# Batch 0 of a fused attention and MLP kernel reworked: head sets and token halves, one PSUM tile placed by hand, W_in products by chunks, a new step order

## Chip, core and metric

The kernel runs on one core of a Trainium2 chip. The metric is the device time of one execution in microseconds (us); less is better. The kernel before took 251.21 us (median of three runs, 250.34 to 251.27).

## What is computed

Eight batches, eight heads, 576 tokens, head width 64, 32 packed rows per head. Inputs are float32, the output is a float32 array of 4608 x 512.

```
def sm_attn(qq, kk, vv):
    s = scale * np.matmul(qq, kk.transpose(0, 1, 3, 2))
    a = np.exp(s - max)
    a = a / (np.sum(a, axis=-1, keepdims=True) + 1e-09)
    return np.matmul(a, vv)
p_packed = sm_attn(p, k, v)              # 32 rows per head
out = sm_attn(q, p_packed, p_packed)     # 576 rows per head
x = out.transpose(0, 2, 1, 3).reshape(4608, 512)
g = s * np.maximum(x @ w_in, 0) ** 2 + b     # w_in 512 x 2048
return g @ w_out                             # w_out 2048 x 512
```

## The kernel before, in words

Everything is computed in bf16 with float32 sums in PSUM. x is never formed: per batch the packed rows (ppd) are multiplied by W_in (tile pw, made by `packed_w`), and the normalised second attention weights (aT) are multiplied by pw, which gives the hidden layer at once.

Per batch the steps are, by the words of the step string: L* loads; T or D transposes (T on TensorE, D by DMA); V reorders V; F the first scores and their exponentials; P the packed rows; X their transposition; S the second scores and exponentials; A the sums, logarithm, inverse and product that give aT; W the product ppd by W_in (16 small matmuls for two chunks of 512 columns, in tiles of 64 x 32 of the array); M (16 per batch, four matmuls of 288 columns each) the hidden layer, relu on ScalarE (ACT) and square on VectorE (DVE); O the output products, 16 matmuls of 512 columns for each 128 tokens, then one DVE instruction and the stores. Batch 0 uses half steps (h, G, E) for its first M. Z and Y are matmuls on zeros that compute nothing (56 in all). BT and BC make the bias row from the column sums of W_out.

The order of every engine is written out by hand: each instruction is pinned to program order, so the step string (lines 660 to 689) and the prologue (633 to 658) fix the order on TensorE (PE), DVE, ACT, GpSimd (POOL) and SyncE (SP). POOL issues the casting loads, SP the stores and the DMA transposes. `mm` is line 62, `tr` line 65, and all of DVE, ACT, POOL and SP go through line 73, so the profile's lines name helpers and tiles tell more.

PSUM before: two pools, `psh` (tag h, two buffers of two banks, `big()`) and `psy` (tag y, four buffers of one bank). A buffer is taken in rotation when the tile is made. Loads of batch 0 (`load`, lines 115 to 122) are cut by heads 0 to 3 and 4 to 7. `first_scores` works on the head sets a = 0 (even heads) and a = 1 (odd heads), so its first half needs both cuts of K. `bias_sums` leaves its four partial rows in biasrep, and `bias_rows` adds them with a float32 matmul.

```
mm(where[a, x][NP * g:NP * g + NP], ppd[b % 2][D * a:D * a + D, a, g, :],
   w_in_sb[D * a:D * a + D, g, ch * NB:(ch + 1) * NB], ..., tile_position=(D * a, NP * g))
```

Of the kernel before, what the change touches and what calls it, by code (L numbers as in the profile page):

```python
# [7 lines left out]
F32 = mybir.dt.float32  # L8
# [6 lines left out]
def kernel(  # L15
# [32 lines left out]
    JJ = NP // 16  # L48

    constp = ctx.enter_context(tc.tile_pool(name="constp", bufs=1))  # L50
    rawp = ctx.enter_context(tc.tile_pool(name="rawp", bufs=1))
    attp = ctx.enter_context(tc.tile_pool(name="attp", bufs=1))
# [5 lines left out]
    psh = ctx.enter_context(tc.tile_pool(name="psh", bufs=2, space=bass.MemoryType.PSUM))  # L58
    psy = ctx.enter_context(tc.tile_pool(name="psy", bufs=4, space=bass.MemoryType.PSUM))
# [17 lines left out]
    early = []  # L77

    def big(dt=F32):
        if early:  # L80
            return early.pop()
        return psh.tile([P, 2, NB if dt == F32 else 2 * NB], dt, tag="h", name="hps")
# [12 lines left out]
    pn = [constp.tile([P, 2, 2, D], BF16, name=f"pn{i}") for i in range(2)]  # L95
    pall = constp.tile([16 * (B - 2), 16, 2, D], BF16, name="pall")
# [10 lines left out]
    rowsf = constp.tile([P, P], F32, name="rowsf")  # L107
# [7 lines left out]
    def load(what, b, h0=0, h1=H):  # L115
        src = {"k": k, "q": q, "v": v}[what]
        if h0 == 0:
            raw[what, b] = rawp.tile([R, H, NC * D], BF16, tag=what + "n", name=what + "n")
        pool.dma_start(
            out=raw[what, b][:, h0:h1, :],  # L120
            in_=src[b, h0:h1].rearrange("h (r c) d -> r h (c d)", c=NC),
        )

# [20 lines left out]

    def load_sb():
        sp.dma_start(out=svec[:], in_=moe_s[0:1].unsqueeze(0).to_broadcast([P, 1]))
        sp.dma_start(out=bvec[:], in_=moe_b[0:1].unsqueeze(0).to_broadcast([P, 1]))
# [6 lines left out]

    def prep_p(b):
        pt = big(BF16)
        for x in range(2):
            tr(
                pt[:, 0, x * P:(x + 1) * P],
                pn[b][:, x, :, :],  # L160
                identb[:],
            )
        for c2 in range(2):
            act.copy(
                out=pbd[D * c2:D * c2 + D, :, b, :, c2, :],
                in_=pt[D * c2:D * c2 + D, 0, 0:2 * P].rearrange("p (g a j) -> p a g j", g=4, a=2),
            )

    def prep_pall():
        n = 16 * (B - 2)  # L170
        pts = [psy.tile([P, 8 * P], BF16, tag="y", name="pps") for _ in range(2)]
# [6 lines left out]
        for x in range(2):  # L178
            src = pts[x][:].rearrange("p (t n) -> p t n", n=P)[:, :, 0:n].rearrange(
                "p t (x a i) -> p a x i t", a=2, i=JJ  # L180
            )
            for c2 in range(2):
                for a in range(2):
                    out = pbd[D * c2:D * c2 + D, a, 2:B, :, c2, :].rearrange(
                        "p b g (i t) -> p (b g) i t", i=JJ
                    )[:, :, :, 8 * x:8 * x + 8]
                    (act.copy if x else vec.tensor_copy)(out=out, in_=src[D * c2:D * c2 + D, a])

    def on_pe(b, what, half):
# [3 lines left out]
        tpw = big(BF16)  # L193
        tp = [tpw[:, 0], tpw[:, 1]]
        split = b == 0 and what == "q"
        if split:
            tp[1] = psy.tile([P, 2 * NB], BF16, tag="y", name="tps")
        for h4 in range(4):
            for cp in range(CP):
                o = (h4 % 2) * HS + cp * R  # L200
                tr(
                    tp[h4 // 2][:, o:o + R],
                    raw[what, b][:, 4 * half + h4, cp * P:(cp + 1) * P],
                    identb[0:R, 0:R],
                )
        d = dst[:, half * 4 * HS:(half + 1) * 4 * HS].rearrange("p (a s) -> p a s", a=2)
        if split:
            act.copy(out=d[:, 0], in_=tp[0][:, 0:2 * HS])
            vec.tensor_copy(out=d[:, 1], in_=tp[1][:, 0:2 * HS])
        else:  # L210
            vec.tensor_copy(out=d, in_=tpw[:, :, 0:2 * HS])
# [8 lines left out]
    def order_v(b, h0=0, h1=H):  # L220
        vec.tensor_copy(
            out=vr[:, :, h0:h1, 0:D].rearrange("r c h d -> r h c d"),
            in_=raw["v", b][:, h0:h1, :].rearrange("r h (c d) -> r h c d", c=NC),
        )

    def first_scores(b, a):
        if a == 0:
            e1[b] = attp.tile([R, 2, NC, 4, NP], BF16, tag="e1", name="e1")
        s1 = big()
        for g in range(4):  # L230
            for cp in range(CP):
# [8 lines left out]
                )  # L240
        act.activation(
# [8 lines left out]
    def packed(b, half=None):  # L250

        if not half:
            pps[b] = psy.tile([P, NB], F32, tag="y", name="pps")
        pp = pps[b][:, 0:2 * DV].rearrange("p (a x) -> p a x", a=2)
        for a in range(2):
            for c in range(NC):
                for g in range(4) if half is None else (2 * half, 2 * half + 1):
# [8 lines left out]
        if half == 0:  # L266
            return
        rd = smp.tile([P, 2], F32, tag="rd", name="rd")
        vec.reciprocal(out=rd[:], in_=pp[:, :, D])
        pk[b] = smp.tile([P, 2, 2, D], BF16, tag="pk", name="pk")  # L270
        for a in range(2):
# [6 lines left out]
    def turned(b):  # L278

        pt = pps[b][:, NB // 2:].bitcast(BF16)  # L280
        for a in range(2):
            tr(pt[:, a * P:(a + 1) * P], pk[b][:, a].rearrange("p c d -> p (c d)"), identb[:])
        vec.tensor_copy(
            out=ppd[b % 2][:].rearrange("p a g j -> p (a g j)"),
            in_=pt[:, 0:2 * P],
        )

    def second_scores(b, by_half=False, with_w=False):
        e2[b] = attp.tile([P, 2, S], BF16, tag="e2", name="e2")
        tiles = [big() for _ in range(2)]  # L290
        for a in range(2):
            for g in range(4):
                for c2 in range(2):
                    t, i = (c2, a) if by_half else (a, c2)
                    mm(
                        tiles[t][NP * g:NP * g + NP, i, 0:HS],
# [6 lines left out]
        if by_half:  # L303
            exp_half(b, tiles, 0, 0)
            exp_half(b, tiles, 1, 0)
            s2[b] = tiles
            return
        if with_w:
            packed_w(b, [0])
        for a in range(2):  # L310
            act.activation(
# [6 lines left out]
    def exp_half(b, tiles, a, hf):  # L318
        act.activation(
            out=e2[b][:, a, hf * HS:(hf + 1) * HS],  # L320
            in_=tiles[hf][:, a, 0:HS],
# [4 lines left out]
    def weights_half(b, hf):  # L326
        if hf == 0:
            aT[b] = atp.tile([P, 2, S], BF16, tag="aT", name="aT")
        dps = big()
        for a in range(2):  # L330
            mm(dps[:, a, 0:HS], onesbd[:], e2[b][:, a, hf * HS:(hf + 1) * HS], start=True, stop=True)
        if hf == 0:
            exp_half(b, s2[b], 0, 1)
            exp_half(b, s2[b], 1, 1)
        ld = smp.tile([P, 2, HS], F32, tag="ld", name="ld")
        act.activation(out=ld[:], in_=dps[:, :, 0:HS], func=AF.Ln)
        rcd[hf] = smp.tile([P, 2, HS], F32, tag="rcd", name="rcd")
        act.activation(out=rcd[hf][:], in_=ld[:], func=AF.Exp, scale=-1.0)

    def weigh_half(b, hf):  # L340
        cols = slice(hf * HS, (hf + 1) * HS)
        vec.tensor_tensor(out=aT[b][:, :, cols], in0=e2[b][:, :, cols], in1=rcd[hf][:], op=ALU.mult)

    def weights(b, a):
        if a == 0:
            aT[b] = atp.tile([P, 2, S], BF16, tag="aT", name="aT")
        dps = big()
        for hf in range(2):
            mm(dps[:, hf, 0:HS], onesbd[:], e2[b][:, a, hf * HS:(hf + 1) * HS], start=True, stop=True)
        ld = smp.tile([P, 2, HS], F32, tag="ld", name="ld")  # L350
        act.activation(out=ld[:], in_=dps[:, :, 0:HS], func=AF.Ln)
        rc = smp.tile([P, S], F32, tag="rcd", name="rcd")
        act.activation(out=rc[:], in_=ld[:].rearrange("p a s -> p (a s)"), func=AF.Exp, scale=-1.0)
        vec.tensor_tensor(out=aT[b][:, a, :], in0=e2[b][:, a, :], in1=rc[:], op=ALU.mult)

    def packed_w(b, chs):
        if b not in pw:
            pw[b] = atp.tile([P, 2, DFF], BF16, tag="pw", name="pw")
        where = {}
        if len(chs) > 1:  # L360
            pair = [big() for _ in range(2)]
            where = {(a, x): pair[a][:, x, :] for a in range(2) for x in range(2)}
        if len(chs) != 2:
            single = [psy.tile([P, NB], F32, tag="y", name="wps") for _ in range(2)]
            where.update({(a, len(chs) - 1): single[a][:] for a in range(2)})
        for x, ch in enumerate(chs):
            for g in range(4):
                for a in range(2):
                    mm(
                        where[a, x][NP * g:NP * g + NP],  # L370
                        ppd[b % 2][D * a:D * a + D, a, g, :],
                        w_in_sb[D * a:D * a + D, g, ch * NB:(ch + 1) * NB],
                        start=True,
                        stop=True,
                        tile_position=(D * a, NP * g),
                    )
        if len(chs) > 1:
            for a in range(2):
                dst = pw[b][:, a, chs[0] * NB:(chs[0] + 2) * NB].rearrange("p (i f) -> p i f", f=NB)
                evict(dst, pair[a][:], a == 0)  # L380
        if len(chs) != 2:
            ch = chs[-1]
            if b == 0 and ch == 0:
                s2["w"] = single
# [336 lines left out]
```

The softmax here doesn't subtract the row's maximum and nothing guards it: scores larger than these inputs give would overflow.

## Time and profile before

| what | value |
| --- | --- |
| time, median of three runs | 251.21 us |
| span of the profiled execution, first to last instruction | 248.04 us (no other time is recorded for that execution; its distance to the median is 3.17 us) |
| busy: PE, DVE, ACT, POOL | 241.6, 144.4, 140.6, 29.1 us |
| granted TensorE clock, mean | 1.000 |
| DMA: bytes, software queue, hardware queue | 35.50 MB, 18.61 MB, 16.49 MB |
| matmuls on zeros | 56 of 2302 |

How to read it: PE is the matmul row and PEld the weight load that overlaps it. A matmul's listed duration (for instance 380 ns for 128x512) includes its way through the array; consecutive ones start closer together, so costs on PE are read from the distance of starts in the timeline. The chain of waits follows the last instruction back to what released each step. A DMA's landing is its issue time on POOL or SP plus the time to landing in the view of DMA issues.

### The profile page before, as it was taken

To read this page: it belongs to the slowest core of one execution; us is meant where nothing else is said; L and a number is where in the kernel's file an instruction comes from. 1 tells how busy PE (TensorE), PEld (TensorE's weight loads), DVE (VectorE), ACT (ScalarE), POOL (GpSimd) and SP (SyncE) were. 2 spreads that over 40 slices of the span, in tenths; PEclk is the share of its full clock that TensorE was granted. 3 is DMA by queue.
4 is the path that set the end of the run, shared out by engine and by line. 5 is a ranking of instruction groups with operands and counts; after the bars stand their busy time and mean duration, and the time that the engine had idled before them with its cause. 6 is when DMAs were issued, how large, how long until landed. Compare 5 with 4: busy or idle time off the path is not lost.

```text
span 248.0 us, 5518 instructions
## 1 busy us (share of the span) xinstructions
PE 241.6 (97%) x2302; PEld 134.2 (54%) x2302; DVE 144.4 (58%) x278; ACT 140.6 (57%) x218; POOL 29.1 (12%) x43
## 2 busy tenths in 40 slices
PE   8999899999999999999999999999999999999994
PEld 2655565356644665456544654466545654366453
DVE  4438875599564864386538753586348742767221
ACT  2266742558837772758555953888266844578000
POOL 8733212000300012000300030000200000000000
PEclk9999999999999999999999999999999999999999
DMA  6999999999696589939798999337998811121133
GB/s 74 174 206 208 201 203 204 197 204 162 136 213 140 140 138 144 225 89 193 115 209 169 160 147 226 85 80 156 146 230 133 185 37 50 42 46 42 42 87 86
DMA packets 59450, 35.50 MB, mean 143 GB/s; under 512 B 32160, under 2 KB 54944, under 8 KB 59424
## 3 DMA queue, kind: packets, MB, share of 16 engines
q0 software_dynamic: 25184, 18.61, 50.8%
q1 hardware_dynamic: 34192, 16.49, 30.2%
q8 instruction: 18, 0.29, 0.5%
q14 instruction: 8, 0.07, 0.1%
q10 hardware_dynamic: 48, 0.03, 0.0%
HBM read 37.23 MB, written 9.44 MB: 188 GB/s over the span
## 4 chain that ended last, share of the span: by engine, by line
PE 82%; DMA 16%; issue 1%; POOL 0%; DVE 0%; POOLq 0%
PE yps L62 49%; PE hps L62 31%; DMA w_out_sb<-in_moe_w_out_dram 14%; DMA kn<-in_k_dram 2%; PE pps L62 1%; PE pps L65 1%; POOL kn L73 0%; DVE ysb L73 0%; POOL identb L73 0%; POOLq L73 0%; POOLq L705 0%
## 5 line engine op out<-in xcount | busy, mean ns | idle before, releaser
L62 PE MATMUL yps<-w_out_sb,gT 128*128 128x512 bf16 (+1 forms) x592 | 147.8, 374 | 0.6 <-DMA w_out_sb<-in_moe_w_out_dram 0.6
L73 ACT ACTIVATE rlu<-hps 128x576 bf16<-128x576 f32 x124 | 77.0, 649 | 23.1 <-PE hps L62 19.9
L62 PEld LDWEIGHTS <-gT 128*128 128x128 bf16 x592 | 54.8, 98 | 50.9 <-issue 8.8
L62 PE MATMUL hps<-aT,pw 128*128 128x288 bf16 x512 | 78.3, 285 | 0.2 <-ACT rlu L73 0.2
L73 DVE TENSOR_TENSOR gT<-rlu 128x576 bf16<-128x576 bf16 x128 | 57.8, 457 | 26.1 <-ACT rlu L73 23.3
L62 PEld LDWEIGHTS <-pw 128*128 128x128 bf16 x512 | 49.7, 97 | 26.3 <-issue 1.2
L73 DVE SCALAR_TENSOR_TENSOR ysb<-yps,svec,biasrep 128x512 f32<-128x512 f32 (+1 forms) x37 | 27.0, 733 | 21.7 <-PE yps L62 21.5
L73 ACT ACTIVATE e<-hps 96x768 bf16<-96x768 f32 (+2 forms) x34 | 21.8, 693 | 30.8 <-PE hps L62 30.6
L73 ACT CAST pw<-hps 128x1024 bf16<-128x1024 f32 x14 | 14.2, 1012 | 21.6 <-PE hps L62 21.0
L73 DVE TENSOR_TENSOR aT<-e,rcd 128x576 bf16<-128x576 bf16 x16 | 12.1, 757 | 23.4 <-ACT rcd L73 23.2
L73 POOL DMA_DIRECT2D kn<-in_k_dram x9 | 6.9, 767 | 130.1 <-DMA kT<-kn 97.8
L73 DVE CAST pw<-hps 128x1024 bf16<-128x1024 f32 x14 | 17.1, 1220 | 4.7 <-PE hps L62 4.6
L62 PE MATMUL zps<-zb 128*128 128x512 bf16 x42 | 13.6, 452 | 1.2 <-DVE zb L73 1.2
L73 ACT ACTIVATE rcd<-ld 128x576 f32<-128x576 f32 x16 | 10.9, 683 | 0.5
L73 ACT ACTIVATE ld<-hps 128x576 f32<-128x576 f32 x16 | 10.3, 643 | 1.2 <-PE hps L62 0.4
L62 PEld LDWEIGHTS <-ppd 64*32 64x32 bf16 x384 | 3.8, 88 | 11.0 <-issue 8.1
L62 PEld LDWEIGHTS <-zb 128*128 128x128 bf16 x56 | 5.6, 108 | 7.2 <-issue 3.2
L73 DVE RECIPROCAL rd<-pps 128x2 f32<-128x2 f32 x8 | 1.4, 171 | 13.3 <-PE pps L62 13.3
L62 PE MATMUL hps<-w_in_sb,ppd 64*32 64x512 bf16 x224 | 8.9, 381 | 0.0
L62 PEld LDWEIGHTS <-kT 128*128 128x128 bf16 x192 | 6.9, 98 | 2.5 <-issue 0.5
L73 DVE COPY vr<-vn 96x3072 bf16<-96x3072 bf16 (+1 forms) x9 | 8.0, 893 | 0.1
L73 POOL DMA_DIRECT2D vn<-in_v_dram x9 | 6.7, 751 | 5.5 <-DVE vr L73 2.9
(58 smaller groups left out, 104.0 us busy)
## 6 DMA issues: line engine op xcount, KB each, us to landing
out_dram<-ysb SPq DMA_DIRECT2D x23, 192.0 KB, 2.6
kn<-in_k_dram POOLq DMA_DIRECT2D x7, 576.0 KB, 7.1
vn<-in_v_dram POOLq DMA_DIRECT2D x7, 576.0 KB, 10.7
qn<-in_q_dram POOLq DMA_DIRECT2D x7, 576.0 KB, 13.3
out_dram<-ysb SPq DMA_DIRECT2D x24, 128.0 KB, 2.4
w_in_sb<-in_moe_w_in_dram POOLq DMA_DIRECT2D x4, 512.0 KB, 14.3
w_out_sb<-in_moe_w_out_dram POOLq DMA_DIRECT2D x4, 512.0 KB, 18.7
out_dram<-ysb SPq DMA_DIRECT2D x23, 64.0 KB, 2.1
```

Source lines behind the costliest of these rows:

```text
L62: return tc.keep_in_program_order(nc.tensor.matmul(*a, **kw))
L65: return tc.keep_in_program_order(nc.tensor.transpose(*a, **kw))
L73: return lambda *a, **kw: tc.keep_in_program_order(f(*a, **kw))
```

## The change

Six parts, made together:

1. **PSUM**: the two pools give way to one tile of eight banks, `banks`, and each step names the bank that it takes behind an @ in the step string. Dependencies are still kept by bank.
2. **Batch 0**: K and V are loaded by head sets (even heads, then odd ones) and Q by token halves (two tiles of 48 partitions); K's transposes, V's reordering, P and X go by sets; Q's transposes, S, the sums, logarithms and products by token half and set. The eight pieces of W_in's product of batch 0 have 256 columns each.
3. **W_in**: its first 256 columns come as float32 on ACT's hardware queue into a buffer of pw and are cast in two parts (C0, C1); P of batch 0 comes as float32 on SP's queue. The other columns come as 512, 256, 512 and 512.
4. **W by chunks**: the product of batches 1 to 7 takes one chunk of 512 columns at a time (8 matmuls, two banks, an eviction of 512 columns on either engine).
5. **Bias**: four partial rows are added by DVE on 32 partitions and scaled into biasrep; the float32 matmul is gone. s and b are loaded by POOL, late.
6. **Order**: a new step string of some 1125 words. Every step with a matmul is begun by one word and carried on by repeated words (a on ACT, v on DVE), so evictions stand apart from the matmuls in it; O has up to four output tiles open at once, and Q is its eviction. 44 matmuls on zeros remain.

```
+    banks = psp.tile([P, 8, NB], F32, name="banks")
+    spots = []
+    def take(n, dt=F32):
+        x = spots.pop(0)
+        t = banks[:, x:x + n, :]
+        return t if dt == F32 else t.bitcast(dt)
...
+    def load_part(what, part):
+        if what == "q":
+            raw["q", 0, part] = rawq.tile([R0, H, NC * D], BF16, tag="qn", name="qn")
...
+            in_={"k": k, "v": v}[what][0].rearrange("(g a) (r c) d -> a r g (c d)", a=2, c=NC)[part],
...
+    def load_w0():
+        wf = atp.tile([P, 2, DFF], BF16, tag="pw", name="pw")
...
+        act.dma_start(out=raw["w"], in_=moe_w_in[:, 0:256].rearrange("(k p) f -> p k f", p=P))
+    def cast_w0(x):
+        to((yield), w_in_sb[:, 2 * x:2 * x + 2, 0:256], raw["w"][:, 2 * x:2 * x + 2])
...
+    def packed_w0(c0, c1):
+        t = take(2)
+        n = c1 - c0
+        for g in range(4):
+            for a in range(2):
+                mm(
+                    t[NP * g:NP * g + NP, a, 0:n],
...
+        for a in range(2):
+            to((yield), pw[0][:, a, c0:c1], t[:, a, 0:n])
...
     def prep_pall():
-        pts = [psy.tile([P, 8 * P], BF16, tag="y", name="pps") for _ in range(2)]
+        pts = [take(1, BF16)[:, 0] for _ in range(2)]
...
-                    (act.copy if x else vec.tensor_copy)(out=out, in_=src[D * c2:D * c2 + D, a])
+                    to((yield), out, src[D * c2:D * c2 + D, a])
...
     def bias_sums():
+        yield
+        vec.tensor_copy(out=bias4[:], in_=ps[0:NP, 0, :])
+        for g in range(1, 4):
+            vec.tensor_tensor(out=bias4[:], in0=bias4[:], in1=ps[NP * g:NP * g + NP, 0, :], op=ALU.add)
+        for g in range(4):
+            vec.tensor_scalar_mul(out=biasrep[NP * g:NP * g + NP], in0=bias4[:], scalar1=bvec[0:NP])
...
-        Lwi0 Lwi1 Lwo0 Lwi2 Lwi3 Lwo1 Lp1 Tk0.0 Z10 PD Tk0.1 Lk1 PP0 Z3 F0.0 V0.0 F0.1 Z5 P0.0 V0.1 Lv1
-        P0.1 Z1 Tq0.0 Z1 X0 Z1 Tq0.1 Lq1 Lwo2 Lwo3 Lpall Z3 S0 Z3 A0.0 Z1 W0.0 A0.1 G0.0 E Y8 h0.0.0
...
+        PD0 C0 Z3@6 PP0@1 PP0a Z7@0 Tk0.0@2 Tk0.0a C0v Lq0.1 Tk0.0a PP0v Z6@0 Tk0.1@4 Tk0.1v Tk0.1a V0.0
+        F0.0@6 F0.1@0 F0.0 F0.1 Lp1 Z2@5 P0.0@2 P0.0 Z3@6 X0.0 X0.0a V0.1 Z1@0 P0.1 P0.1 Z1@0 Tq0.0@3,4
+        Tq0.0v Tq0.0v X0.1 Z2@0 Tq0.1@3,5 Tq0.1a C1 C1v S0.0.0@6 X0.1v S0.0.1 e0.0 PD1 e0.1 PP1@4 W0.0@0
+        Tq0.1v S0.1.0@2 S0.1.1 PP1v PP1v e1.1 Z2@5 d1.1@4 W0.0v e1.0 d0.1@6 l1.1 i1.1 d0.0 Lwi2.4 d1.0
+        l1.0 i1.0 Lwi1.2 W0.0v W0.3@0 W0.3v l0.0 Z4@2 W0.1@2 W0.3v W0.2@4 G1.1 l0.1 i0.0 G1.0 Z1@0
+        h0.6.1@0 W0.1a W0.2a W0.1v h0.2.1@6 W0.2v h0.6.1v i0.1 h0.0.1@2 h0.2.1a Lwi4.6 G0.0 G0.1 h0.0.1a
+        Lwi6.8 W0.5@4 W0.5v W0.5a Lk1 Lv1 h0.6.1 h0.2.1 h0.0.1 W0.4@0 W0.4v h0.2.0@6 h0.2.0a h0.10.1@2
...
+        Tq1.1a Tq1.1v W1.0@2 S1@6,4 W1.0a W1.0v Lsb S1 W1.1@0 W1.1v W1.1v W1.3@2 h0.4.0 PA O0.0x1@6
+        h0.8.1 S1 O0.1x1@7 O0.0x3 A1.1@4 W1.3v W1.3a O0.2x1@0 A1.1 O0.2x1 O0.3x2@1 A1.1 Lk2 O0.3x1
+        O0.2x1 A1.1 PPA0@4,5 O0.1x1 Lwo8.12 A1.0@2 PPA0v O0.1x1 PPA0a O0.0x3 PPA0v O0.2x1 O0.3x1 PPA0v
+        O0.3x1 A1.0 W1.2@2 O0.2x1 PPA0v A1.0 h0.12.1 Dk2 PPA0a PPA0v PPA0a W1.2a O0.3x2 A1.0 M1.3@4
+        M1.3a W1.2v O0.1x1 O0.2x1 M1.11@2 M1.9@4 M1.11a M1.9v O0.2x1 Lwo12.16 M1.9 Lv2 O0.1x3 M1.3
+        M1.0@2 M1.0a M1.10@4 M1.10a M1.11 O0.0x1 Lq2 O0.2x1 BT@2 M1.2@4 M1.2a O0.2x4 M1.0 O0.2x2 M1.14@4
+        O0.2x1 M1.14a BT Dq2 O0.1x3 F2.0@2 F2.0 O0.3x1 F2.1@4 F2.1 V2 O0.3x2 M1.2 Lq3 O0.2x1 Q0.2 M1.6@2
...
```

## Prediction

> **What bounds the kernel now.** I read the page first: busy shares, slices, clock and chain.
>
> ```profile
> span 248.0 us, 5518 instructions
> ...
> PE 241.6 (97%) x2302; PEld 134.2 (54%) x2302; DVE 144.4 (58%) x278; ACT 140.6 (57%) x218; POOL 29.1 (12%) x43
> ...
> PE   8999899999999999999999999999999999999994
> ...
> PEclk9999999999999999999999999999999999999999
> ...
> PE yps L62 49%; PE hps L62 31%; DMA w_out_sb<-in_moe_w_out_dram 14%; DMA kn<-in_k_dram 2%; PE pps L62 1%; PE pps L65 1%; POOL kn L73 0%; DVE ysb L73 0%; POOL identb L73 0%; POOLq L73 0%; POOLq L705 0%
> ```
>
> PE is the bound, full in every slice, at full clock. But 14% of the chain is the load of W_out: PE's early work ends up waiting for DMA. So what counts is when useful work starts, what PE issues, and when W_out is there. Next the timeline of PE up to 50 us.
>
> ```profile
> 1.19 5.30 PE L62 MATMUL zps<-zb 128*128 128x512 bf16 x12 [1.19 <-DVE zb L73]
> ...
> 20.37 0.65 PE L62 MATMUL hps<-aT,pw 128*128 128x288 bf16 x4
> ...
> 27.85 0.41 PE L62 MATMUL wps<-w_in_sb,ppd 64*32 64x512 bf16 x8 [0.57 <-DMA w_in_sb<-in_moe_w_in_dram]
> ...
> 42.35 0.59 PE L62 MATMUL yps<-w_out_sb,gT 128*128 128x512 bf16 x2 [0.57 <-DMA w_out_sb<-in_moe_w_out_dram]
> ...
> 44.89 1.05 PE L62 MATMUL hps<-w_out_sb,onesb 128*32 128x512 bf16 x16
> 45.87 0.42 PE L62 MATMUL hps<-e,onesbd 128*128 128x288 bf16 x2
> ...
> 47.47 1.10 PE L62 MATMUL hps<-biasrep,rowsf 128*128 128x512 f32 x2
> 48.40 1.03 PE L62 MATMUL yps<-w_out_sb,gT 128*128 128x512 bf16 x4
> ```
>
> The first M stands at 20.37; two waits for loads follow; BT, which needs all of W_out, ends at 45.87 (the start of the next matmul). From there PE never rests. Last, the end, in the chain of waits:
>
> ```profile
> 239.81 4.80 PE yps L62 x38
> 244.61 0.03 issue
> 244.63 0.48 DVE ysb L73
> ```
>
> By single records the last O begins near 244.45. So I split at BT: time = BT's end + work left behind it + tail. The profiled span is 248.04 and the median 251.21; the 3.17 us between are added unchanged.
>
> **Work behind BT.** Before it is 244.45 - 45.87 = 198.58 us. PE costs are distances of starts: a 128x512 matmul .2156 (16 of O: ysb's inputs are ready 3.45 apart), four of 288 columns .49 (60.05 to 60.54), a transpose of 96 columns .0425, a sum (ones) .123. What stands after BT in the new order, against the old:
> - 20 matmuls of M fewer (done earlier): 5 x .49 = -2.45; two of O more: +.43.
> - 16 transposes of Pall and two sums fewer: -.68 - .25.
> - BC is gone: 48.40 - 47.47 = -.93.
> - Four chunks of W fewer (done earlier), and the rest stand by threes or beside S. A pair takes .57, a single .34, so an adjacent chunk adds .23. 14 x .57 = 7.98 becomes 6 x .80 + 6 x .23 = 6.18: -1.80.
> - Fewer switches into small tiles, 26 to 18, each about .09 by these rows:
>
> ```profile
> 72.13 1.47 PE L62 MATMUL yps<-w_out_sb,gT 128*128 128x512 bf16 x6
> 73.53 0.67 PE L62 MATMUL hps<-w_in_sb,ppd 64*32 64x512 bf16 x16
> 74.13 1.47 PE L62 MATMUL yps<-w_out_sb,gT 128*128 128x512 bf16 x6
> ```
>
> Six of O are 1.29, yet W starts 1.40 later: .11 here, .09 over several places. 8 x .09 = -.72.
>
> Sum -6.4. Against it a new wait: the bias is now eight DVE instructions, no longer four and a matmul. The trace has none of 32x512; the bounds are .34 (a 256-column cast's cadence) and .75 (a 512-column ysb), so .68 + 3 x .75 + 4 x (.35 to .75) = 4.3 to 5.9 us, standing ahead of V2 in DVE's order. P2.1 on PE waits for V2, and O and M of the next tiles stand behind P2.1. Lowest price 0 (the M's and O's between cover it), highest 1.2; I take .5. The three PSUM pairs of M come back after 1.47 us (three M's) and need about 1.44 (matmuls, two hops of .2, a relu of .65, .1 back), so they cost tenths, counted there. Left behind BT: 198.58 - 6.4 + .5 = **192.7**.
>
> [...]
>
> **BT's end.** The new order, by the same unit costs from the trace:
> - First M. Twelve zero matmuls are gone, warm cost 12 x .2156 = 2.6, but they only filled waits. The chain instead: zeros until 6.29; transposes of K's first set (12, .51) after 8.6, its second set until 10.9 (landings of K as before, 5.9 and 8.5, same bytes by the same queue); scores and exponentials (two of .70) until 13.2; packed rows 14.5 and X; Q's halves land at 13.5 and 14.6, their transposes take 48 of 48 columns (between 1.02 and 2.04 us by half and whole a 96-column transpose, I take 1.4) until 17.4; S with four exponentials until 19.2; sums, and four dependent ACT steps of 288 columns (.41) to 20.95; product and hop: first M at **21.5**, against 20.37. So no earlier: ACT's chain, not zeros, sets it.
> - From there to the first O, PE has 64 of M 7.8, four W0 pieces .7, transposes of K1 and Q1 2.0, scores .7, P and X .6, three chunks .9, S .4: 13.1 us. DVE has more: 14 squares x .373 = 5.2, seven casts of 256 columns x .342 = 2.4, three relus x .755 = 2.3, V1 .95, two aT products .75, four copies to kT and qT 1.6, P1's small ones .6, two W1 casts 1.4: 15.2. Before, DVE was filled in the same stretch too:
>
> ```profile
> 21.00:38.00 17.00, 16.15 (x159) 10.04 (x157) 14.18 (x28) 10.42 (x19) 3.55 (x5) 1.00 1.29 204
> ```
>
> (length, then PE, PEld, DVE, ACT, POOL busy; clock; DMA share). Bounds: 15.2 if DVE is never idle, 18.2 if it is filled 83% as there; I take 16.4, nearer the full one since its inputs are spread over three PSUM pairs. First O at 37.9.
> - To BT's end: 30 of O 6.5, 20 of M 2.45, W chunk .3, sums .5, Pall's transposes .7, BT 1.0 = 11.4; waits .9 (0 to 1.9: the Pall copies share one bank and alternate between ACT and DVE, before all of one half went to one engine). **50.2**.
> - Loads: the last quarter of W_out must land. Before it landed at 44.4 (issue 25.32 plus 19.1), with Pall and k2 behind it; now they stand ahead, so it takes the place of k2, which landed at 48.6 (issue 35.05 plus 13.5). BT reads it in its last quarter, so DMA allows an end of 48.7 to 49.4: just hidden.
>
> Other edits at nothing: loads by sets and halves carry the same bytes; 256 columns of W_in as float32 take the DMA engines about as long as the cast did (packets of 1 KB 47 ns against 98), and their casts (.35 to .7 each) lie in DVE's and ACT's idle time before 17 us, else X0.1 is up to .7 late; s and b are needed first at BT; SP's stores stand behind the transpositions of K2 and Q2, covered by the five output buffers. If that cover were gone, O would stop for the 2.4 to 3.6 us that one occupies SP.
>
> The removed zeros touch the clock. The trace shows a granted clock of 1.00 throughout and only the first twelve matmuls at double price, .43 apart; the longest single wait in my chain is under 1.9 us, and I put no price on it. [...]
>
> **Sum.** 50.2 + 192.7 = 242.9 for the last O; before's tail of 248.04 - 244.45 = 3.59, +.2 as the last stores are issued together on SP (.3 to .6 each): span 246.7; + 3.17 = **249.9 us**. Each us of BT's end is one us of time: equal at about 51.5.
>
> **Rivals.**
> - R1, the waits before the first O don't come (DVE 15.2 or less, as ACT takes its share): BT's end falls to what the loads allow, 48.7: 248.4. For: ACT is idle 39% of 21 to 38. Against: DVE's 14.18 busy there. Chance .25.
> - R2, the gain is used up: Pall's copies serialise on their bank (BT's end 51.2), and V2 behind the bias and PSUM cost 1.3, not .5: 251.7. The change would then not do what it says, no net work being won. Chance .17.
> - R3, the other side: the last quarter of W_out lands late, at 52.4. Before, loads moved a steady 200 GB/s; a transposition of K2 by DMA now runs beside it, and each of the loads ahead waits for its buffer. It decides from a BT end of 51.5 on; at 53.1 the time is 252.8. Against: k2 landed at 48.6 and leaves 3 us. Chance .13.
> - The forecast, 249.9, has .45; its terms, BT's end from 49.6 to 50.8, give 249.3 to 250.5.
>
> A measurement of this kernel can tell some 0.5% from no change, so faster means below 249.95, slower above 252.47. The forecast falls .26 faster, .19 same; R1 .25 faster; R2 .16 same, .01 slower; R3 .13 slower: **.51, .35, .14**. The range, 247.6 to 252.6, takes in the forecast, R1 to .8 below its price (a landing at 47.9), and R2; what lies out is most of R3 and a little below, under .2.
>
> **What would show it.** First M at 21.5 (earlier: Q's price was too high); DVE near full from 21.5 to 38; BT's end near 50 and what released it (PE's own order: forecast; DMA w_out_sb: R3); P2.1 idle behind V2 up to 1.2; 30 groups of tiled matmuls; the last O near 242.9. Wrong makes it above all a DVE that leaves PE waiting for several us before the first O, a late quarter of W_out, or a slow clock in the first 20 us.

## The result and the profile after

The changed kernel takes **257.89 us** (median of four runs, 257.41 to 258.90) against 250.79 for the kernel before, measured beside it: 1.0295 times, interval 1.0265 to 1.0325. So 3% slower, where 249.9 was forecast and 252.6 was the end of the range. An execution more than 1.5% above the fastest of its kernel counts for a median but not for a ratio. The profiled execution took 258.27 us with a span of 256.50; the 1.77 us around the span (1.77 to 1.81 in every later execution that has both numbers) stand where the prediction, with no such pair at hand, had added 3.17. The span of 248.04 that it started from is shorter than that of every timed execution of the kernel before (248.6 to 249.6), so the other 1.4 us were the distance to slower executions.

The page of the changed kernel, the lines that answer to those of the kernel before:

```profile
span 256.5 us, 5695 instructions
...
PE 238.4 (93%) x2327; PEld 136.2 (53%) x2360; DVE 157.7 (61%) x323; ACT 129.5 (50%) x228; POOL 29.8 (12%) x44
...
PE   8979989773999999999999999999999999999993
...
PEclk9997999997799999999999999999999999999998
...
PE banks L64 73%; DMA kT<-kn 7%; PE banks L67 0%; DVE ysb L75 0%
```

PE is busy for 3 us less, which doesn't show by itself that its work shrank (the row has 2327 matmuls for 2360 weight loads, so 33 records are missing, and part of the rest ran at half clock), and the span is 8.5 us longer: three slices of 6.4 us between 45 and 64 us fall to 7, 7 and 3 tenths, and the granted clock, full throughout before, dips in three slices of the first 71 us. The load of W_out is gone from the chain; K's transposition stands in its place.

The waits of PE, the longest first (total, times, longest one):

```profile
PE banks L64 <- DMA kT<-kn: 5.4, 1, 5.4
PE banks L64 <- issue: 3.0, 12, 1.1
PE banks L64 <- DVE aT L75: 1.7, 1, 1.7
```

and where they stand in PE's timeline:

```profile
19.11 0.24 PE L64 MATMUL banks<-qT,ppd 64*32 64x144 bf16 x4 [1.10 <-issue]
...
23.67 1.63 PE L64 MATMUL banks<-aT,pw 128*128 128x288 bf16 x12
...
51.99 1.05 PE L64 MATMUL banks<-w_out_sb,onesb 128*32 128x512 bf16 x16
52.97 0.66 PE L64 MATMUL banks<-aT,pw 128*128 128x288 bf16 x4
...
55.47 0.81 PE L64 MATMUL banks<-w_out_sb,gT 128*128 128x512 bf16 x3
61.67 0.82 PE L64 MATMUL banks<-pbd,kT 128*128 128x64 bf16 x12 [5.39 <-DMA kT<-kn]
```

The first M starts at 23.67 (21.5 forecast), BT ends at 52.97 (50.2), and 3 us later the first scores of batch 2 (F2.0) stand still for 5.39 us. SP's timeline and the tile's landing tell why:

```profile
43.54 7.44 SPq L75 DMA_TRANSPOSE kT<-kn  x1
```

```profile
DMA to landing us min/median/max: 18.1/18.1/18.1
```

K of batch 2 had landed and its transposition was issued at 43.54, and it took 18.1 us. Before the change F2.0 stood at 67.05 us, and the transposition, issued at 59.33 with no load in flight, landed in 5.4:

```profile
59.33 3.45 SPq L73 DMA_TRANSPOSE kT<-kn  x1
```

```profile
DMA to landing us min/median/max: 5.4/5.4/5.4
```

The new order asks for K2 at 56.3, eleven us earlier, and the transposition runs beside the last half of W_out, v2 and q of batches 2 and 3, which land between 45.9 and 61.7. The DMA queues between 50 and 56 us after the change:

```profile
DMA packets 2280, 1.14 MB, mean 191 GB/s; under 512 B 1170, under 2 KB 2280, under 8 KB 2280
...
q0 software_dynamic: 1138, 0.85, 90.5%
q1 hardware_dynamic: 1142, 0.29, 36.5%
```

In these 6 us the loads (q0) moved 1138 packets and the transposition (q1) 1142, almost the same number. But by these rows a load's packet carries some 750 bytes and the transposition's some 250, so the transposition moves 48 GB/s of the 191.

The clock, in the windows view (length; PE, PEld, DVE, ACT, POOL busy; clock; DMA share; GB/s), cut at the bounds that the trace's clock records give:

```profile
16.14:19.55 3.41, 2.15 (x69) 1.39 (x69) 2.85 (x9) 1.44 (x4) 1.77 (x3) 1.00 1.32 202
19.55:22.96 3.41, 3.41 (x17) 1.08 (x16) 1.49 (x4) 3.09 (x9) 1.50 (x2) 0.50 1.26 211
60.51:67.34 6.83, 5.33 (x81) 3.29 (x83) 1.35 (x4) 2.26 (x3) 2.31 (x3) 0.50 1.04 159
```

Half clock from 19.55 to 22.96, behind the wait of 1.10 us, and from 60.51 to 67.34, behind the wait for K2. Of the latter 5.67 us lie after F2.0's start, so some 2.8 us of work were lost.

### The profile page after: what moved, and what is told of

Its sections match the earlier page's. It is cut to its first block, busy times and chain, and to the rows that moved or that the text cites. A ratio compares the mean times of both kernels' runs of the same rounds, so it can differ in the third digit from the quotient of the medians.

```text
span 256.5 us, 5695 instructions
## 1 busy us (share of the span) xinstructions
PE 238.4 (93%) x2327; PEld 136.2 (53%) x2360; DVE 157.7 (61%) x323; ACT 129.5 (50%) x228; POOL 29.8 (12%) x44
## 4 chain that ended last, share of the span: by engine, by line
PE 73%; DMA 7%; issue 1%; DVE 0%
PE banks L64 73%; DMA kT<-kn 7%; PE banks L67 0%; DVE ysb L75 0%
## 5 line engine op out<-in xcount | busy, mean ns | idle before, releaser
L64 PE MATMUL banks<-w_out_sb,gT 128*128 128x512 bf16 (+1 forms) x562 | 136.2, 375 | 2.6 <-issue 1.8
L75 ACT ACTIVATE rlu<-banks 128x576 bf16<-128x576 f32 x109 | 64.4, 660 | 30.5 <-PE banks L64 26.7
L64 PE MATMUL banks<-aT,pw 128*128 128x288 bf16 x512 | 73.5, 287 | 1.9 <-DVE aT L75 1.7
L75 DVE TENSOR_TENSOR gT<-rlu 128x576 bf16<-128x576 bf16 x128 | 55.4, 455 | 13.1 <-ACT rlu L75 8.6
L75 DVE SCALAR_TENSOR_TENSOR ysb<-banks,svec,biasrep 128x512 f32<-128x512 f32 (+1 forms) x37 | 26.9, 733 | 46.3 <-PE banks L64 39.6
L75 ACT ACTIVATE e<-banks 96x768 bf16<-96x768 f32 (+2 forms) x34 | 21.9, 693 | 46.8 <-PE banks L64 46.8
L75 DVE CAST pw<-banks 128x512 bf16<-128x512 f32 (+1 forms) x41 | 24.2, 613 | 9.3 <-PE banks L64 9.1
L75 DVE TENSOR_SCALAR rlu<-banks 128x576 bf16<-128x576 f32 x19 | 14.2, 754 | 4.6 <-PE banks L64 1.8
L75 ACT CAST pw<-banks 128x512 bf16<-128x512 f32 (+1 forms) x31 | 15.4, 565 | 0.9 <-PE banks L64 0.8
L64 PE MATMUL banks<-zb 128*128 128x512 bf16 x41 | 13.8, 475 | 1.4 <-DVE zb L75 1.2
L75 DVE TENSOR_TENSOR aT<-e,rcd 128x576 bf16<-128x576 bf16 (+1 forms) x18 | 11.8, 684 | 0.7 <-ACT rcd L75 0.6
L75 ACT ACTIVATE rcd<-ld 128x576 f32<-128x576 f32 (+1 forms) x18 | 10.8, 630 | 0.2
L75 DVE RECIPROCAL rd<-banks 128x2 f32<-128x2 f32 (+1 forms) x9 | 1.5, 169 | 10.9 <-PE banks L64 10.9
```

The source lines that it names most:

```text
L64: return tc.keep_in_program_order(nc.tensor.matmul(*a, **kw))
L75: return lambda *a, **kw: tc.keep_in_program_order(f(*a, **kw))
```

## The experiments

My theory (A): K2's transposition beside loads, and the half clock that such a wait leaves behind, are the loss. The rivals: the wait only covers another one (B); the transposition is slow for a reason of its own on SP (C); zeros do not hold the clock (D). Of diffs of the step string only the words around the edit are shown. Unless said otherwise, times are medians, and a ratio is to the kernel before, measured beside each (250.40 to 250.58).

**K2 on TensorE.**

```
-  h0.12.1 Dk2 PPA0a PPA0v PPA0a W1.2a O0.3x2 A1.0 M1.3@4 M1.3a W1.2v
+  h0.12.1 PPA0a PPA0v PPA0a W1.2a O0.3x2 A1.0 Tk2.0@4 Tk2.0a W1.2v Tk2.0a Tk2.1@2 Tk2.1v Tk2.1a M1.3@4 M1.3a
```

> The changed kernel, with one edit: K of batch 2 is transposed by TensorE (24 small matmuls and four copies of the kind used for batch 1), not by a DMA transposition. Theory A (the loss is the 5.4 us wait of F2.0 for that transposition, which lands 18.1 us after its issue because the loads run beside it, and the half clock that follows it, 6.8 us of which 5.7 fall on work, so 2.8 lost): 258 - 5.4 - 2.8 + 1.0 for the transposes = about 251; a point above if S2 now waits for the DMA transposition of Q2. Theory B (the wait covers something that would be late anyway: V2 behind the eight bias instructions, or PSUM): F2.0 starts on time but P2.1 waits in its place, 255 or more.

252.55 us (251.39 to 253.25), ratio 1.0078 (1.0054 to 1.0103): 5.3 us of the 7 come back (about 251 was expected). F2.0 follows BT without a wait, P2.1 waits only .6 us for V2, so B falls. Its profiled execution still has two spells of half clock of 3.41 us, at 18.56 and at 49.28; one of its six executions has full clock throughout and is the fastest, 251.39.

**q of batch 3 loaded later.**

```
-  M1.2 Lq3 O0.2x1
+  M1.2 O0.2x1
...
-  X2v O0.1x1 Lk3
+  X2v O0.1x1 Lk3 Lq3
```

> The changed kernel, with one edit: the load of q of batch 3 is issued behind that of k of batch 3, so that it cannot run beside K2's transposition. Theory A (loads and the transposition share the DMA engines): one load of 576 KB less in front of it at some 142 GB/s is 4 us; the transposition lands near 57.5 instead of 61.6, the wait of F2.0 falls from 5.4 to 1 to 1.5 us and the clock keeps its full rate: 251 to 253. Theory C (the transposition is slow for another reason, its late or long issue on SP, 7.4 us instead of 3.5 in the kernel before): it lands near 61.6 as it does now, 258.

253.35 us, ratio 1.0090 (1.0055 to 1.0124). K2's landing in this kernel:

```profile
DMA to landing us min/median/max: 15.1/15.1/15.1
```

One load less in front makes it 3.0 us quicker, where A had 4 and C nothing; F2.0 starts at 58.61 but, as the head came out faster, still waits 4.6 us (1 to 1.5 expected). So only .8 us of the gain of 4.5 is the wait; BT ends 2.3 us earlier and the half clock behind the wait lasts 3.41 us instead of 6.83. In this execution the clock did not fall in the head, and the first M stands at 21.35 and BT ends at 50.72: the prediction's 21.5 and 50.2, within half a microsecond.

**Zeros in the head.**

```
-  e0.1 PP1@4 W0.0@0 Tq0.1v S0.1.0@2
+  e0.1 PP1@4 W0.0@0 Z4@2 Tq0.1v S0.1.0@2
```

> The changed kernel, with one edit: four more zero matmuls ahead of the second half of batch 0's second scores (at about 17.9 us), where TensorE stood still for 1.1 us and the clock fell to half from 19.55 to 22.96. Theory A (the fall comes from too little TensorE work in the window before it): the clock stays at 1.00 there, first M 1 to 1.7 us earlier (23.7 now), time 256.2 to 257. Theory D (the fall has another cause, or the stall moves behind the zeros): the fall remains and the zeros cost up to .9 us: 258 to 259.

257.45 us. The fall in the head is gone; the windows view of this kernel:

```profile
17.31:20.73 3.42, 3.23 (x68) 1.69 (x65) 2.19 (x8) 2.01 (x5) 2.85 (x4) 1.00 1.30 200
```

From the last zero matmul ahead of the second packed rows (P0.1) to the first M it takes 8.40 us (13.96 to 23.67 = 9.71 in the changed kernel; 8.24 in the run above, whose clock did not fall). So the fall costs 1.3 to 1.5 us and the four zeros next to nothing. The time moved by only .4, for two reasons: the head of this execution began .6 us later, and what it won before BT it waited longer for K2 (5.9 us).

**The kernel before without zeros.**

```
-  Lpall Z3 S0 Z3 A0.0 Z1 W0.0 A0.1 G0.0 E Y8 h0.0.0
+  Lpall S0 A0.0 W0.0 A0.1 G0.0 E h0.0.0
```

> The kernel before, without the 15 zero matmuls between 15.5 and 20.4 us (Z3 ahead of S0, Z3 and Z1 behind it, Y8 ahead of the first M). Theory A (they hold the clock): a window of 3.41 us at half clock between 17 and 25 us, up to 1.7 us lost there, of which the later waits for loads (0.6 us each at 27.8 and 42.3) take some back: 251 to 252.5. Theory D (they only fill time in which TensorE waits): no window at half clock, first M up to 0.5 us earlier, 250.3 to 251.2.

252.88 us, four executions from 250.27 (mean clock .998) to 253.76 (.980), ratio 1.0102 (1.0063 to 1.0142). The profiled one is the fastest, with no fall; the other three have mean clocks of .980 to .986, where none of the kernel before's fell below .993. So these zeros hold the clock, and whether it falls without them changes from execution to execution; the worst case is above the range that I gave.

**A gate ahead of the loads.** POOL copies two elements of K2's tile before it goes on:

```
+        elif what == "GK":
+            pool.tensor_copy(out=gate[:], in_=kT[b % 2][0:1, 0:2])
...
-  O0.0x1 Lq2 O0.2x1 BT@2
+  O0.0x1 O0.2x1 BT@2
...
-  BT Dq2 O0.1x3 F2.0@2
+  BT O0.1x3 F2.0@2
...
-  M1.2 Lq3 O0.2x1
+  M1.2 GK2 Lq2 Dq2 O0.2x1
...
-  X2v O0.1x1 Lk3
+  X2v O0.1x1 Lk3 Lq3
```

> The changed kernel, with one edit on the DMA side: POOL first copies two elements of K2's transposed tile (so it waits for that transposition) and only then issues the loads of q of batches 2 and 3 and k of batch 3; the transposition of Q2 follows its load. Theory A (sharing with loads makes the transposition late; with q3 alone put off it landed 3 us earlier): it now runs beside the rest of W_out and v2 only and lands near 54.5 on a timetable where F2.0 is due at 53.7 to 56; the wait falls below 1.5 us from 5.4, no half clock follows it; 250 to 251.5. Against it: Q2 lands near 66 and S2, due near 65, may wait 1 to 2 us. Theory C (the issue on SP is what is slow): wait of 3 us or more as before, 253 or more.

261.55 us, ratio 1.0443: slower than the change itself, and yet it speaks for A. K2, issued at 43.80, lands 10.8 us later, at 54.6 as expected, and F2.0 no longer waits. The wait comes back at S2, larger; PE's waits in this kernel:

```profile
PE banks L64 <- DMA qT<-qn: 7.6, 1, 7.6
```

The loads of k3 and q3, held back, and v3 now run beside the transposition of Q2, which is issued at 61.20 and takes 12.8 us.

**Pall's copies parted by engine**, with the gate:

```
-  PPA0v O0.1x1 PPA0a O0.0x3 PPA0v O0.2x1 O0.3x1 PPA0v O0.3x1 A1.0 W1.2@2 O0.2x1 PPA0v A1.0 h0.12.1 Dk2 PPA0a PPA0v PPA0a
+  PPA0v O0.1x1 PPA0v O0.0x3 PPA0v O0.2x1 O0.3x1 PPA0v O0.3x1 A1.0 W1.2@2 O0.2x1 PPA0a A1.0 h0.12.1 Dk2 PPA0a PPA0a PPA0a
```

> The kernel with the gate, and with the eight copies of Pall's transposes given as before the change: the four that read the one bank all to VectorE, the four of the other all to ScalarE. If the bank that ScalarE and VectorE share in turn is what delays aT of batch 1, the wait of 1.7 us ahead of batch 1's first M falls to below 1 us and the time by about 1 us: 249 to 250.5. If VectorE is simply full there, the wait stays between 1.5 and 2.

261.72 us (249 to 250.5 expected): no gain in time, since Q2 decides it, and with the faster head F2.0 waits 2.8 us for K2 again. But among PE's waits that for aT, ahead of batch 1's first M, is .3 us instead of 1.7:

```profile
PE banks L64 <- DVE aT L75: 0.3, 1, 0.3
```

So the copies as the change gave them cost 1.4 us before BT. In the changed kernel VectorE waits .54 and .17 us for ScalarE's copies of the same banks, and ScalarE 1.29, .42 and .63 for VectorE's; here neither waits for the other. But the edit also takes one copy of .5 us from VectorE (five become four), so not all of the 1.4 us is shown to be the bank.

**With the zeros too** (Z4@2 as above):

> As the last, with the four zero matmuls ahead of the second half of batch 0's second scores. If the clock's falls in the first 25 us come by too little work in a window of 3.41 us, they go, and the runs lie closer together: 249 to 250 with a spread under 1 us (about 2 us without the zeros). If not, as the last and up to .5 more.

263.36 us, a miss by 13 us in time: Q2's wait is 11 us here. The head has no fall, nor had the run before it.

**K2's transposition early in the kernel before.**

```
-  Lq2 X1 O0.2x5 O0.0x2
+  Lq2 X1 Dk2 O0.2x5 O0.0x2
...
-  M1.3 Dq2 Dk2 Lk3
+  M1.3 Dq2 Lk3
```

> The kernel before, with one edit: the DMA transposition of K2 is issued some 11 us earlier, as soon as k2 has landed (about 48.6), beside the loads of v2 and q2, instead of on an empty queue at 59.3. Theory A (loads beside it slow it): from issue to landing 8 to 11 us instead of 5.4. Theory C: about 5.5 as before. F2.0 comes at 67, so the time stays 250 to 251.3 by both.

251.21 us in its one run. From issue to landing 8.1 us instead of 5.4, beside v2 and q2; and Q2's own, now beside loads of batch 3 that start sooner, takes 12.3 instead of 6.5. The effect is there without any other part of the change.

**A second gate**, on Q2, ahead of k and q of batch 3 (with the first gate and the parted copies):

```
+            pool.tensor_copy(out=gate[:], in_=qT[b % 2][0:1, 0, 0, 0:2])
-  GK2 Lq2 Dq2
+  GK2 Lq2 Dq2 GQ2
```

> The kernel with the gate and Pall's copies parted by engine, and with a second gate: POOL waits for the transposition of Q2 before it loads k and q of batch 3. Theory A (a transposition lands in 5 to 6 us on a quiet queue and in 11 to 18 beside loads): Q2's lands in about 6 us instead of 12, near 67, the wait of 7.6 to 9 us ahead of S2 falls to 0 to 1; K2's wait of 2 to 3 us stays: 251 to 253. Theory C (its time does not depend on the loads): the wait ahead of S2 stays 7 or more, 260.

253.13 us, ratio 1.0080. Q2's transposition, issued at 63.2 in both kernels, takes 4.9 us from issue to landing where it took 12.3 with one gate and the copies parted:

```profile
DMA to landing us min/median/max: 12.3/12.3/12.3
```

```profile
DMA to landing us min/median/max: 4.9/4.9/4.9
```

The wait ahead of S2 is 2.5 us (0 to 1 expected, 7 or more by C). C falls: the same instruction at the same time is fast or slow by what is loaded beside it.

**The losses repaired**: K2 on TensorE and the copies parted; then also seven zeros (Z4@2 as above, and Z3@7 ahead of X1).

> The changed kernel with K2 transposed by TensorE, and Pall's copies parted by engine. Theory A (the losses of the change are K2's transposition, the shared bank and the clock that falls in their wake): 1.2 us below the kernel with K2 on TensorE alone (252.55), one fall of the clock less (up to 1.7): 249.5 to 251.3. Theory B (something else holds the new order back): as that kernel, 252 to 253.

> As the last, with four zero matmuls ahead of the second half of batch 0's second scores and three ahead of X1 (where TensorE waits .7 us for VectorE). Theory A: the clock no longer falls in the first 60 us in most runs, and the zeros stand in waits: 248.8 to 250, runs within 1 us of each other. Theory D (the falls are not stopped by zeros, or the zeros are on the path): 250.5 or more.

251.11 us (250.34 to 251.49), ratio 1.0005 (.9991 to 1.0020); and with zeros 250.76 (250.47 to 251.02), ratio 1.0004 (.9994 to 1.0015). The zeros halve the spread and keep the mean clock at .996 or more, in all twelve executions. The waits of PE in the latter, all that are left above .2 us:

```profile
PE banks L64 <- DVE zb L75: 1.2, 1, 1.2
PE banks L64 <- DVE vr L75: 0.6, 1, 0.6
PE banks L64 <- DMA qT<-qn: 0.4, 1, 0.4
PE banks L64 <- ACT kT L75: 0.3, 1, 0.3
```

So the loss is explained and undone. But the gain is missing: 248.8 to 250 was expected for the last one, and it is level with the kernel before. By its time that is D's range (250.5 or more), although the falls did stop.

**F2 put later**, K2's DMA transposition kept, with the gate on Q2, the parted copies and the seven zeros:

```
-  BT Dq2 O0.1x3 F2.0@2 F2.0 O0.3x1 F2.1@4 F2.1 V2 O0.3x2 M1.2 Lq3 O0.2x1 Q0.2 M1.6@2
-  M1.6a P2.1@4 P2.1 M1.14 O0.3x4 M1.8@2 X2 X2v O0.1x1 Lk3 O0.3x1 M1.8a O0.3x1 M1.4@4 M1.1@2 O0.1x1
-  M1.10 O0.1x1 M1.6 Q0.3 M1.4v M1.1a M1.8 M1.13@0 M1.5@2 M1.5a M1.4 M1.1 M1.7@4 M1.7v M1.7 O0.1x3
-  M1.13a M1.13 W2.3@2
+  BT Dq2 GQ2 O0.1x3 O0.3x1 V2 O0.3x2 M1.2 O0.2x1 Q0.2 M1.6@2 M1.6a M1.14 O0.3x4 M1.10 M1.8@4 M1.8a O0.1x1
+  O0.3x2 M1.6 M1.4@2 M1.4v Q0.3 M1.8 M1.13@0 M1.13a O0.1x1 F2.0@4 F2.0 M1.4 M1.1@2 M1.1a F2.1@4 F2.1 M1.13 M1.1
+  M1.5@0 M1.5a O0.1x1 Lk3 Lq3 M1.7@2 M1.7v M1.5 M1.7 P2.1@4 P2.1 O0.1x3 X2 X2v W2.3@2
```

> The changed kernel with the DMA transposition of K2 kept, but what needs it put later: the first scores and packed rows of batch 2 stand behind some 5 us more of M and O work of batch 0 and 1, POOL loads k and q of batch 3 only after Q2's transposition has landed; with Pall's copies parted by engine and the seven zero matmuls. Theory A (the new order merely asks for K2 before a transposition beside loads can land): F2.0 comes near 59 and waits less than 1 us, Q2 may cost another 1; nothing else changes, so the last output matmul is near 243 and the time 249 to 250, below the kernel before. Theory B (the pulled-forward order itself is what gains, and putting F2 back gives it up): waits at S2 or ahead of batch 2's first M of 2 us and more, 251 to 253.

253.14 us, ratio 1.0096. K2 is no longer waited for, BT ends at 50.21, but my order made new waits: 1.7 us for the eviction of bank 1 (M1.13 too early), 1.1 at X2, and .4 twice, and the clock was at half from 59.8 to 63.2. Neither 249 to 250 nor B's waits at S2 came.

**The bias off VectorE.** Is it VectorE's block of eight bias instructions (4.75 us) that holds the repaired kernels back? On ScalarE for copy and scalings (first with K2 on TensorE, then with F2 late, M1.13 and P2.1 mended):

```
-        vec.tensor_copy(out=bias4[:], in_=ps[0:NP, 0, :])
+        act.copy(out=bias4[:], in_=ps[0:NP, 0, :])
-            vec.tensor_scalar_mul(out=biasrep[NP * g:NP * g + NP], in0=bias4[:], scalar1=bvec[0:NP])
+            act.mul(out=biasrep[NP * g:NP * g + NP], in_=bias4[:], mul=bvec[0:NP])
```

> The changed kernel with K2 on TensorE, Pall's copies parted by engine and seven zero matmuls (250.76), and five of the eight instructions that make the bias row (the copy and the four scalings) on ScalarE. Theory E (the block of 4.75 us on VectorE is a cost of its own): V2 comes some 2.5 us earlier, the wait of P2.1 for it (.6 us) goes, and 250.0 to 250.3 results. Theory F (TensorE does not feel the block): 250.6 to 251.

> The kernel with the first scores of batch 2 late (253.14), with five of the eight bias instructions on ScalarE, M1.13 no longer ahead of the eviction of its bank, and P2.1's evictions ahead of a square. Theory E (the block on VectorE, and in its wake the squares and relus, made the waits of 1.7, 1.1, .4 and .4 us there): they fall to 1 us in all, no fall of the clock behind them, last output matmul near 243: 248.8 to 250. Theory F: waits of 2 us or more remain between the bias sums and S2, 251 or more.

254.35 and 253.09 us, outside what E expected, but inconclusive: on ScalarE the copy stood behind two relus and came 3 us late, and PE waited for the bank that the sums read, 2.5 us in the first of the two.

Only the four scalings on GpSimd (vec to pool in the last line):

> The changed kernel with K2 on TensorE, Pall's copies parted by engine and seven zero matmuls (250.76), and the four scalings of the bias on GpSimd. Theory E (the block on VectorE is a cost): V2 comes 1.95 us earlier, the wait of P2.1 (.6 us) goes: 250.0 to 250.3. Theory F: no difference, 250.6 to 250.9; or slower, if GpSimd takes so long that the first output tile waits for the bias.

> The changed kernel with the first scores of batch 2 late (253.14 in its first form), M1.13 and P2.1 mended, Pall's copies parted, seven zero matmuls, and the four scalings of the bias on GpSimd. Theory E: the squares and with them the relus come 2 us earlier, the waits between the bias sums and S2 (3.6 us in the first form) fall to 1 us and the clock holds: 249 to 250.3. Theory F: waits of 2 us or more remain: 251 or more.

255.68 and 256.15 us: a miss. GpSimd's timeline in the first of them:

```profile
55.05 7.40 POOL L75 TENSOR_SCALAR biasrep<-bias,bvec 32x512 f32<-32x512 f32 x4 [16.16 <-DVE bias L75]
```

1.85 us for each, against .48 on VectorE, so the first output tile waited for the bias, and TensorE 4.7 us for what stood behind that tile in VectorE's order (X2's input). The wait of P2.1 for V2 (.6) was gone.

**The scalings behind V2**, nothing moved between engines (K2 on TensorE); and behind three squares (F2 late):

```
+        yield
         for g in range(4):
             vec.tensor_scalar_mul(out=biasrep[NP * g:NP * g + NP], in0=bias4[:], scalar1=bvec[0:NP])
-  F2.1@4 F2.1 V2 O0.3x2
+  F2.1@4 F2.1 V2 BT O0.3x2
```

and for the late order, from BT on:

```
+  BT Dq2 GQ2 O0.1x3 O0.3x1 M1.2 M1.14 M1.10 O0.3x2 BT O0.2x1 M1.6@2 M1.6a Q0.2 O0.3x4 M1.8@4 M1.8a O0.1x1 O0.3x2
+  M1.6 Q0.3 V2 M1.4@2 M1.4a M1.8 O0.1x1 M1.13@0 M1.13a F2.0@4 F2.0 M1.4 F2.1@2 F2.1 O0.1x1 M1.1@4 M1.1a M1.13
+  M1.5@0 M1.5v M1.1 Lk3 Lq3 M1.7@2 M1.7a P2.1@4 P2.1 M1.5 O0.1x3 M1.7 X2 X2v W2.3@2
```

> The changed kernel with K2 on TensorE, Pall's copies parted by engine and seven zero matmuls (250.76), with the four scalings of the bias on VectorE behind V2 and not ahead of it. Theory E: the wait of P2.1 for V2 (.6 us) goes and nothing replaces it: 250.0 to 250.3. Theory F: the wait goes but Q0.2 or a square comes later in its place: 250.6 to 251.

> The changed kernel with the first scores of batch 2 late, the squares of three M's ahead of the bias scalings and V2 behind them, M1.13 and P2.1 mended, Pall's copies parted, seven zero matmuls, k and q of batch 3 loaded behind Q2's transposition. Theory E: no wait above .7 us between the bias sums and S2 but up to 1 us for K2's transposition, the last output matmul near 243.5: 249 to 250.3, at or below the kernel before. Theory F: waits of 2 us or more remain: 251 or more.

The first takes 256.59 us, twelve executions from 251.04 to 259.27, ratio 1.0103 (1.0060 to 1.0147, from three of them): a miss. The wait for V2 is gone. But V2 reads v2's buffer 2.4 us earlier, so POOL loads v3 earlier, at 56.09 instead of 58.53, beside the transposition of Q2, which takes 13.1 us instead of 10.9. PE's wait at S2, in the execution with a trace (254.34 us; what the slower ones waited for isn't shown):

```profile
67.32 0.44 PE L64 MATMUL banks<-qT,ppd 64*32 64x288 bf16 x16 [2.71 <-DMA qT<-qn]
```

The last one takes 250.98 us (250.13 to 251.65), ratio 1.0008 (.9996 to 1.0021): 2.2 us less than the first late order, no wait above .7 us behind the first 2 us, and again level with the kernel before. The waits that theory E named are gone, but M1.13 and P2.1 were mended in the same step, so how much of the 2.2 us belongs to the bias isn't shown, and the time is above E's 249 to 250.3. No version beats the kernel before.

## Why the prediction was wrong, point by point

Starts on PE in us, single records:

| | before | forecast | after | q3 later | K2 on PE, copies, zeros | F2 late, last form |
| --- | --- | --- | --- | --- | --- | --- |
| first M | 20.37 | 21.5 | 23.67 | 21.35 | 22.78 | 23.20 |
| first O | 30.62 | 37.9 | 39.49 | 37.24 | 38.66 | 39.09 |
| end of BT | 45.87 | 50.2 | 52.97 | 50.72 | 52.31 | 51.20 |
| F2.0 | 67.05 | - | 61.67 | 58.61 | 55.46 | 59.42 |
| last O | 244.32 | 242.9 | 252.22 | 248.12 | 244.61 | 244.59 |
| span | 248.04 | 246.7 | 256.50 | 252.30 | 248.99 | 248.84 |

- **The failed step: the work behind BT was summed, but nobody asked when it could start.** The sum takes off M's, W's and BC and adds .5 us for V2, as if F2.0 could stand wherever the string puts it. It had no line for K2, which F2.0 needs. The rows gave a warning, not a price: the landing of 5.4 was seen with no load in flight, and in the new order loads run beside it. Behind BT it was 252.22 - 52.97 = 199.25 instead of 192.7: 5.39 of wait and some 2.8 of half clock on top of 191.1.
- **The size of the work was right.** Those 191.1 us, and 192.3 with K2 on TensorE (244.61 - 52.31), lie on both sides of 192.7. The bias took 4.75 us on VectorE (4.3 to 5.9 forecast), and with K2 on TensorE V2's wait was .6 (.5 forecast).
- **R3 named the pair and chose the wrong victim.** It let the transposition of K2 delay W_out's last quarter. W_out came in time (BT waited for nothing); the transposition, whose 1142 packets carried .29 MB between 50 and 56 us where the loads' 1138 carried .85, took 18.1 us and was the one that lost.
- **The clock was waved through.** "The longest single wait in my chain is under 1.9 us, and I put no price on it" cost 1.3 to 1.5 us in the head. It did so in some executions only: two of the changed kernel's four have the mean clock of .987 that the kernel with four zeros shows with no fall in the head, and took 257.41 and 257.52, the others .977 and .980 with 258.27 and 258.90. The wait there was 1.10 us: the clock fell behind a gap of 1.33 us between two matmuls, in a window of 3.41 us with 2.15 us of PE work. So the zeros that were removed did have a price.
- **Up to BT**: first M +2.2, the stretch of VectorE 15.8 instead of 16.4, the last stretch 13.5 instead of 12.3. Against the kernel with q3 later, whose first M came at 21.35, 1.5 us arose behind the last zero ahead of P0.1 (the fall, and a wait of 1.10 instead of .67) and .85 ahead of it, where the clock's first rise came at 5.90 instead of 3.94. R2's mechanism is seen in the last stretch: Pall's copies, 1.4 us.
- **The constants.** The tail behind the last O is 4.3 us instead of 3.8, and the time around the span 1.77 instead of 3.17. The last O of before begins at 244.32, not 244.45 as the prediction read it; that moves .13 us from the work to the tail and leaves the sum. In all: +2.8 at BT, +6.5 behind it, +.5 tail, -1.4 around the span, 8.4 us from 249.9 to 258.3.
- **Where the gain went.** With the losses repaired, BT ends 5.3 to 6.4 us later than before, what is left behind it is 5.1 to 6.1 us shorter (192.3 and 193.4 against 198.5), and the tail is .5 to .7 us longer. The windows view, cut at BT's end, of the kernel before and of the one with F2 late in its last form (stretch, length, then PE, PEld, DVE, ACT, POOL busy; clock; DMA share; GB/s), both at full clock:

```profile
0.00:45.87 45.87, 43.00 (x487) 23.92 (x487) 27.11 (x64) 22.20 (x38) 17.63 (x28) 1.00 1.22 182
45.87:244.30 198.43, 198.33 (x1819) 110.28 (x1816) 116.82 (x213) 118.39 (x181) 11.47 (x15) 1.00 0.73 136
```

```profile
0.00:51.20 51.20, 48.66 (x622) 26.69 (x622) 35.87 (x91) 32.12 (x62) 18.06 (x29) 1.00 1.27 188
51.20:244.60 193.40, 191.60 (x1750) 108.47 (x1746) 120.25 (x229) 97.98 (x168) 11.70 (x16) 1.00 0.75 132
```

  Behind BT TensorE has 6.7 us less to do, close to the 6.4 forecast, but ahead of it 5.7 us more: in all 1.1 us less, about the five zeros by which the two kernels differ. Idle time (1.4 us more) and the tail take more than that back. So the parts moved work across BT and took hardly any away. No run isolates BC or the chunks of W, so what each of them is worth isn't shown.
- **The wait of 1.10 us** ahead of the last four matmuls of S0 has one companion in the traces. Queue q8, which the page calls instruction, loads 16 KB at a time, its first load begins at 16.87 us in the changed kernel, and the wait ends 2.24 us later. In all 17 traced executions of the new order these four matmuls start 2.19 to 2.47 us after the start of that load, with a wait ahead of them or with zeros in its place. That these matmuls wait for that load is my reading of the two standing together; no run moves the load, so it isn't shown.

## What to carry to other kernels

When an order is pulled forward, make a timetable of the loads and DMA transpositions that the moved steps need, beside the sum of work: what was hidden may have been hidden only because it was late (K2's transposition, 5.4 us before and 18.1 after). The time of a DMA transposition depended here on what was loaded beside it (4.9 or 12.3 us for the same one, of Q2; 1142 packets to the loads' 1138 for that of K2); hold loads back, or have TensorE transpose, but then look at the next transposition too: when v2's buffer came free 2.4 us earlier, v3 was loaded earlier, and Q2's transposition beside it took 13.1 us instead of 10.9. Zeros that fill waits were not free to remove (252.88 us without 15 of them, 250.40 with them): price the clock.

## What the runs showed of the hardware

- The clock changed at whole multiples of 3.413 us from one another: in the changed kernel at 5.90, 19.55, 22.96, 60.51 and 67.34 (4, 1, 11 and 2 times apart), and with K2 on TensorE it fell at 18.56 and 49.28 (9 times). Where the changes stand differs from execution to execution: the first rise came between 3.9 and 7.2 us. Where it came later, the head came later: the last zero ahead of P0.1 stands at 13.11 with a rise at 3.94 (q3 later), at 13.96 with one at 5.90 (the changed kernel) and at 14.60 with one at 7.20 (K2 on TensorE, copies, zeros). The kernel before is not free of falls either: with K2 transposed early the clock rose at 3.90 and was at half again from 7.31 to 10.72, and its own executions with a mean clock of .993 took 251.1 to 251.4 us, all others 250.3 to 250.6.
- The windows of 3.41 us ahead of the falls held from 0 to 2.76 us of PE's busy time (0 ahead of 60.51 in the changed kernel, 2.42 ahead of 18.56 with K2 on TensorE, 2.76 with two gates, ahead of 17.84); others were not followed by a fall with as little as 1.65 (44.62 to 48.03 in the changed kernel with four zeros) and 1.75 (4.97 to 8.38 in the kernel before without zeros). So the sum of busy time isn't the measure; what is, the runs do not tell.
- A transposition of 576 KB by DMA took 4.3 to 6.5 us with no load in flight (4.3 at 166.42 in the changed kernel, 6.5 at 56.30 in the kernel before). With loads in flight that of K2 took 8.1 us (kernel before, K2 transposed early) to 18.1 us (changed kernel, with five of them, which moved 3123 packets in that time). Two of later batches in the changed kernel took 9.7 us (issued at 139.46, 1044 packets of two loads beside it) and 15.7 us (at 110.30, 2352 packets of three); one issued at 90.85 took 4.5 us, with two loads issued before it landed but no packet of theirs beside it.
